# The last 256 columns of a sparse-weight matmul's output, stored in one transfer or in three

## The chip, the cores and the metric

The kernel runs on one core of a Trainium2 chip. The metric is the device time of one execution in microseconds (us). Three runs of the kernel before are at hand, and a profile of one execution.

## The reference

The weight matrix is pruned 2:4: in every group of four consecutive rows, and for each column, the two entries of largest magnitude stay and the others become zero. Then a dense layer with bias is computed for 16 x 512 = 8,192 tokens of 1,024 features.

```python
B, S, D = 16, 512, 1024             # x: [B, S, D], w: [D, D], b: [D], all bfloat16
wg = w.reshape(D // 4, 4, D)
mag = jnp.abs(wg)
order = jnp.argsort(mag, 1)
thr = jnp.take_along_axis(mag, order[:, 2:3, :], 1)
wp = (wg * (mag >= thr)).reshape(D, D)
return jnp.einsum("bsd,df->bsf", x, wp) + b
```

## The kernel before, in words

The tokens are cut into 64 tiles of 128. A tile's output is [128 tokens, 1024 columns], made in two halves of 512 columns (`FH`), each in a PSUM bank of its own; eight banks are used in turn (`next_bank`). The contraction over 1,024 features takes eight matmuls per half (`KT` = 8).

There are two stages. The front, up to line 312, runs an order written out by hand in the string `FRONT`: it loads the weights in pieces (`load_w`, line 71) and the first tokens (`load_x`, line 79) over the DMA queues of SyncE (SP in the profile, DMA queue q1) and ScalarE (ACT, DMA queue q10), prunes the weights on VectorE, and computes the first 14 tiles partly while the weights are still coming in. The main loop (line 328) then walks over batches of tiles. The tokens of a batch come from memory through a transposing DMA issued from SP (`issue_batch`, line 242), two batches ahead. Each tile takes sixteen matmuls (line 338), and VectorE adds the bias as it moves each half from PSUM to SBUF (`evac_dve`, line 219). Two tiles make a pair, and ScalarE's queue stores each finished pair with one transfer of 512 KB (`half_done`, line 199); tile 62 is stored by itself.

The last tile, 63, goes through `last_tile` (lines 317 to 326). It makes its output in four pieces, each with eight matmuls (`mm_nat`, line 234) and one bias add (line 323): columns 0 to 511, 512 to 767, 768 to 895 and 896 to 1023. The output collects in one SBUF tile, `o_last`. When 768 columns are there, ScalarE's queue stores them (line 325, 128 rows of 1,536 bytes, 192 KB). After the last piece SP's queue stores the remaining 256 columns (line 326, 128 rows of 512 bytes, 64 KB).

`K` keeps every instruction in the order in which it is written. The framework gives each transfer one of eight semaphores in rotation, and at the end of the program SP waits for all of them, and for VectorE's and ScalarE's own, before the engines meet in a closing barrier; these instructions carry line 368, the end of the program. The profile shows waits inside an engine's queue under names such as SPq and ACTq.

Of the kernel before, what the change touches and what calls it, by code (L numbers as in the profile page):

```python
# [10 lines left out]
def kernel(  # L11
# [7 lines left out]
    nc = tc.nc  # L19
    P = 128  # L20
# [5 lines left out]
    K = tc.keep_in_program_order  # L26
# [10 lines left out]
    of = out.flatten_outer_dims()  # L37
# [15 lines left out]
    def next_bank():  # L53
        bk = nbk[0] % 8
        nbk[0] += 1
        return bk
# [175 lines left out]
    def mm_nat(t, h, bk, c0=0, c1=FH):  # L232
        for kt in range(KT):
            K(nc.tensor.matmul(bank[bk][:, :c1 - c0], lhsT=xN[t][:, kt, :], rhs=wp_nat[h][:, kt, c0:c1],  # L234
                               start=kt == 0, stop=kt == KT - 1))
# [80 lines left out]

    def last_tile(t):
        o_sb = const.tile([P, Dout], bf16, name="o_last")
        for h, c0, c1 in ((0, 0, FH), (1, 0, 256), (1, 256, 384), (1, 384, FH)):
            bk = next_bank()  # L320
            mm_nat(t, h, bk, c0, c1)
            f = slice(h * FH + c0, h * FH + c1)
            K(nc.vector.tensor_tensor(o_sb[:, f], bank[bk][:, :c1 - c0], bias_sb[:, f], op=Alu.add))  # L323
            if f.stop == 768:
                K(nc.scalar.dma_start(of[t * P:(t + 1) * P, :768], o_sb[:, :768]))
        K(nc.sync.dma_start(of[t * P:(t + 1) * P, 768:], o_sb[:, 768:]))

    for bi, (t0, nb) in enumerate(batches):
        if bi + 2 < len(batches):
            issue_batch(*batches[bi + 2])  # L330
        for t in range(t0, t0 + nb):
            if t == NT - 1:
                last_tile(t)
                continue
            bks = (next_bank(), next_bank())
            for kt in range(KT):
                for h in range(2):
                    K(nc.tensor.matmul(bank[bks[h]][:], lhsT=xN[t][:, kt, :], rhs=wp_nat[h][:, kt, :],  # L338
                                       start=kt == 0, stop=kt == KT - 1))
            for _ in range(4 if t == T + F else 3):  # L340
                if later:
                    add_bias(*later.pop(0))
            for h in range(2):
                evac_dve(t, h, bks[h])
# [28 lines left out]
```

## Time and profile before

| | |
|---|---|
| three runs, median (lowest to highest) | 233.83 us (233.76 to 233.94) |
| profiled execution: span from first to last instruction | 231.53 us |
| profiled execution: its own device time | not on the page; the runs' median lies 2.30 us above the span |
| granted TensorE clock | 1.00 throughout |
| 192 KB store of line 325: issue, time to landing | 228.26 us, 1.9 us |
| 64 KB store of line 326: issue, time to landing | 229.01 us, 1.7 us |

The span counts from the first instruction to the last. What lies outside it belongs to the device time but not to the trace. "Time to landing" runs from the issue of a transfer to the last rise of its semaphore. A transfer of this kernel is spread over 16 DMA engines; each moves its share as packets, one per row, and closes with a packet of 4 bytes that raises the transfer's semaphore by one. The trace has a record of every packet with its queue, its start, its length and its size, but not with its DMA engine.

### The profile page before, as it was taken

How to read it: one execution, taken by the hardware profiler on the slowest of the kernel's cores; microseconds unless marked ns; L12 is line 12 of the kernel's file. 1: busy time of each engine (PE TensorE's matmuls, PEld its weight loads, DVE VectorE, ACT ScalarE, POOL GpSimd, SP SyncE). 2: the span in 40 equal slices, each digit the busy share in tenths (PEclk: the TensorE clock that was granted, in tenths of full speed). 3: DMA queues.
4: the chain of work that ended last, by engine and by line, in shares of the span. 5: the costliest groups of instructions: out<-in, count | busy, mean ns of one | idle time of the engine just before them, and what ended most of it. 6: DMA issues, size and time to landing. Idle time of an engine off the chain costs nothing.

```text
span 231.5 us, 2724 instructions
## 1 busy us (share of the span) xinstructions
PE 226.3 (98%) x1128; PEld 110.6 (48%) x1147; DVE 119.9 (52%) x204; ACT 18.8 (8%) x34; POOL 0.7 (0%) x6
## 2 busy tenths in 40 slices
PE   7999999999999999999999999999999999999995
PEld 3887444444444444444444444444444444444443
DVE  4899887867987424424424423423433433433433
ACT  3977500000000000000000000000000000000000
POOL 1000000000000000000000000000000000000000
DMA  6999889999847221995239822696129991122222
GB/s 194 319 200 242 190 178 178 253 246 296 295 181 272 91 83 34 239 201 172 93 75 238 230 93 91 120 258 197 63 91 197 188 249 46 47 91 91 91 93 91
DMA packets 76972, 38.19 MB, mean 165 GB/s; under 512 B 62752, under 2 KB 68896, under 8 KB 76960
## 3 DMA queue, kind: packets, MB, share of 16 engines
q1 hardware_dynamic: 67696, 20.91, 45.2%
q10 hardware_dynamic: 9264, 17.11, 20.4%
q8 instruction: 9, 0.15, 0.3%
q14 instruction: 3, 0.02, 0.0%
HBM read 3.41 MB, written 16.78 MB: 87 GB/s over the span
## 4 chain that ended last, share of the span: by engine, by line
PE 96%; DMA 2%; issue 1%; SPq 0%; DVE 0%
PE bank L338 73%; PE bank L182 16%; PE bank L234 6%; DMA xh<-in_x_dram 2%; PE bank L161 0%; SPq L79 0%; SPq L71 0%; DVE o_last L323 0%
## 5 line engine op out<-in xcount | busy, mean ns | idle before, releaser
L338 PE MATMUL bank<-wp_nat,xTb 128*128 128x512 bf16 x737 | 161.7, 379 | 0.8
L219 DVE TENSOR_TENSOR o_pair<-bank,bias_sb 128x512 bf16<-128x512 f32 x104 | 67.3, 686 | 99.6 <-PE bank L338 94.2
L338 PEld LDWEIGHTS <-xTb 128*128 128x128 bf16 x752 | 73.6, 98 | 88.7
L210 DVE TENSOR_TENSOR stage<-bank,stage 128x512 f32<-128x512 f32 x22 | 14.4, 686 | 3.9 <-PE bank L182 3.8
L182 PE MATMUL bank<-w,xT 128*128 128x256 bf16 x128 | 14.3, 273 | 0.0
L214 DVE TENSOR_TENSOR o_pair<-stage,bias_sb 128x512 bf16<-128x512 f32 x22 | 14.0, 682 | 0.0
L182 PE MATMUL bank<-wp_nat,xg 128*128 128x512 bf16 x62 | 13.9, 379 | 0.1
L182 PEld LDWEIGHTS <-xT 128*128 128x128 bf16 x128 | 12.5, 98 | 1.4
L206 ACT COPY stage<-bank 128x512 f32<-128x512 f32 x22 | 11.4, 618 | 3.9 <-PE bank L182 3.9
L182 PE MATMUL bank<-wp_nat,xfill 128*128 128x512 bf16 x47 | 10.6, 379 | 0.1
L234 PE MATMUL bank<-wp_nat,xfill 128*128 128x512 bf16 x47 | 10.5, 379 | 0.1
L182 PEld LDWEIGHTS <-xg 128*128 128x128 bf16 x64 | 6.3, 98 | 7.6
L234 PEld LDWEIGHTS <-xfill 128*128 128x128 bf16 x48 | 4.7, 98 | 5.7
L182 PEld LDWEIGHTS <-xfill 128*128 128x128 bf16 x48 | 4.7, 98 | 5.5
L338 PE MATMUL bank<-wp_nat,xTs 128*128 128x512 bf16 x32 | 7.1, 379 | 0.0
L142 DVE TENSOR_TENSOR mask<-mag,thr 128x512 bf16<-128x512 bf16 (+2 forms) x8 | 5.4, 690 | 0.2
L144 DVE TENSOR_TENSOR w<-w,mask 128x512 bf16<-128x512 bf16 (+2 forms) x8 | 5.3, 688 | 0.1
L103 PE MATMUL bank<-zeros 128*128 128x512 bf16 (+1 forms) x11 | 4.0, 533 | 1.2 <-DVE zeros L96 1.2
L338 PEld LDWEIGHTS <-xTs 128*128 128x128 bf16 x32 | 3.1, 98 | 3.8
L166 ACT COPY xT<-bank 128x512 bf16<-128x512 bf16 x8 | 4.1, 607 | 2.7 <-PE bank L161 2.7
L118 DVE TENSOR_SCALAR mag<-w 128x512 uint16<-128x512 uint16 (+2 forms) x5 | 2.3, 477 | 2.7 <-DMA w<-in_w_dram 2.7
L234 PE MATMUL bank<-wp_nat,xTb 128*128 128x128 bf16 (+2 forms) x32 | 3.7, 272 | 0.0
(20 smaller groups left out, 26.9 us busy)
## 6 DMA issues: line engine op xcount, KB each, us to landing
out_dram<-o_pair ACTq DMA_DIRECT2D x31, 512.0 KB, 2.8
wp_nat<-w SPq DMA_DIRECT2D x16, 128.0 KB, 2.8
w<-in_w_dram SPq DMA_DIRECT2D x3, 512.0 KB, 6.0
xh<-in_x_dram SPq DMA_DIRECT2D x3, 256.0 KB, 4.5
xh<-in_x_dram ACTq DMA_DIRECT2D x1, 256.0 KB, 4.0
w<-in_w_dram SPq DMA_DIRECT2D x1, 256.0 KB, 5.1
bias_sb<-in_b_dram SPq DMA_DIRECT2D x2, 128.0 KB, 3.7
out_dram<-o_pair ACTq DMA_DIRECT2D x1, 256.0 KB, 2.0
```

Of the source, the lines that this page charges most:

```text
L103: K(nc.tensor.matmul(bank[7][:, :n], lhsT=zeros[:, :P], rhs=zeros[:, :n], start=True, stop=True))
L118: K(nc.vector.tensor_single_scalar(mag[:, ms].bitcast(u16), w_of(i)[:, ms].bitcast(u16), 0x7FFF, op=Alu.bitwise_and))
L142: K(nc.vector.tensor_tensor(mask[:, ms], mag[:, ms], tb, op=Alu.is_ge))
L144: K(nc.vector.tensor_tensor(w_of(i)[:, ms], w_of(i)[:, ms], mask[:, ms], op=Alu.mult))
L166: K(nc.scalar.copy(xt[:], src))
L182: K(nc.tensor.matmul(dst, lhsT=lhs, rhs=rhs, start=c0 == 0 and m == 0, stop=c1 == FH and m == 3))
L206: K(nc.scalar.copy(stage[(h, t)][:], bank[own[(h, t)]][:]))
L210: K(nc.vector.tensor_tensor(st, bank[own[(2 + h, t)]][:], st, op=Alu.add))
L214: K(nc.vector.tensor_tensor(get_o(t)[:, f], stage.pop((h, t))[:], bias_sb[:, f], op=Alu.add))
L219: K(nc.vector.tensor_tensor(get_o(t)[:, f], bank[bk][:], bias_sb[:, f], op=Alu.add))
L234: K(nc.tensor.matmul(bank[bk][:, :c1 - c0], lhsT=xN[t][:, kt, :], rhs=wp_nat[h][:, kt, c0:c1], start=kt == 0, stop=kt == KT - 1))
L338: K(nc.tensor.matmul(bank[bks[h]][:], lhsT=xN[t][:, kt, :], rhs=wp_nat[h][:, kt, :], start=kt == 0, stop=kt == KT - 1))
```

## The change

The store of the last 256 columns, one transfer of 128 rows by 512 bytes from SP, becomes three. Columns 768 to 895 are stored from SP as soon as the third bias add is done (128 rows of 256 bytes, 32 KB). Columns 896 to 1023 are stored after the fourth bias add by two transfers of 64 tokens each (64 rows of 256 bytes, 16 KB), tokens 0 to 63 from SP and tokens 64 to 127 from ScalarE. The store of the first 768 columns stays. The matmuls, the bias adds and everything ahead of the last tile are the same.

```diff
     def last_tile(t):
         o_sb = const.tile([P, Dout], bf16, name="o_last")
+        rows = of[t * P:(t + 1) * P, :]
         for h, c0, c1 in ((0, 0, FH), (1, 0, 256), (1, 256, 384), (1, 384, FH)):
             bk = next_bank()
             mm_nat(t, h, bk, c0, c1)
             f = slice(h * FH + c0, h * FH + c1)
             K(nc.vector.tensor_tensor(o_sb[:, f], bank[bk][:, :c1 - c0], bias_sb[:, f], op=Alu.add))
             if f.stop == 768:
-                K(nc.scalar.dma_start(of[t * P:(t + 1) * P, :768], o_sb[:, :768]))
-        K(nc.sync.dma_start(of[t * P:(t + 1) * P, 768:], o_sb[:, 768:]))
+                K(nc.scalar.dma_start(rows[:, :768], o_sb[:, :768]))
+            elif f.stop == 896:
+                K(nc.sync.dma_start(rows[:, 768:896], o_sb[:, 768:896]))
+        for eng, q in ((nc.sync, slice(0, P // 2)), (nc.scalar, slice(P // 2, P))):
+            K(eng.dma_start(rows[q, 896:], o_sb[q, 896:]))
```

## The prediction

> **What bounds the kernel now.** I read the busy table first, then the chain of work that ended last, then the end of the span in the timeline, then the stretches after the last compute instruction, then the end-of-program waits, and last two places where both DMA queues were at work.
>
> The page's busy table and its chain by engine:
>
> ```profile
> PE 226.3 (98%) x1128; PEld 110.6 (48%) x1147; DVE 119.9 (52%) x204; ACT 18.8 (8%) x34; POOL 0.7 (0%) x6
> PE 96%; DMA 2%; issue 1%; SPq 0%; DVE 0%
> ```
>
> TensorE is busy for 226.3 of 231.53 us. The diff touches no matmul and no vector instruction, so only the end can move. The chain's last pieces and the timeline there (start, length, engine, line):
>
> ```profile
> 225.16 3.51 PE bank L234 x32
> 228.67 0.02 issue
> 228.69 0.29 DVE o_last L323
> ...
> 228.26 0.35 ACTq L325 DMA_DIRECT2D out_dram<-o_last  x1
> 228.69 0.29 DVE L323 TENSOR_TENSOR o_last<-bank,bias_sb 128x128 bf16<-128x128 f32 x1 [0.15 <-PE bank L234]
> 229.01 0.35 SPq L326 DMA_DIRECT2D out_dram<-o_last  x1
> ```
>
> The last bias add ends at 228.985 and SP issues the last store at 229.013. Between them and the end of the span stand 2.52 us, cut here by the store's packets (stretch, length, engines' busy time, clock, DMA share, GB/s):
>
> ```profile
> 229.01:229.86 0.84, 0.00 (x0) 0.00 (x0) 0.00 (x0) 0.00 (x0) 0.00 (x0) 1.00 0.64 233
> 229.86:230.21 0.36, 0.00 (x0) 0.00 (x0) 0.00 (x0) 0.00 (x0) 0.00 (x0) 1.00 0.63 184
> 230.21:230.70 0.49, 0.00 (x0) 0.00 (x0) 0.00 (x0) 0.00 (x0) 0.00 (x0) 1.00 0.00 0
> 230.70:231.53 0.83, 0.00 (x0) 0.00 (x0) 0.00 (x0) 0.00 (x0) 0.00 (x0) 1.00 0.00 0
> ```
>
> 0.84 us pass from issue to first packet (the busy DMA there is still ScalarE's 192 KB store), 0.36 us from the first packet to the end of the last, 0.49 us until SP sees the landing, 0.83 us for the closing barrier. The change can reach the first three, 1.69 us, and the order of the waits behind them:
>
> ```profile
> L368 SPq EVENT_SEMAPHORE  x7: 17/28/28, 229.4 to 231.5; - x7
> SPq L368 <- DMA out_dram<-o_last: 1.1, 2, 0.6
> ```
>
> By the operands in the trace's instruction records, SP's first five of these seven wait for two semaphores each: 104 and 103 (at 229.406), 107 and 102 (229.475), 108 and 100 (229.537), 109 and VectorE's (230.165), 110 and ScalarE's (230.703). Transfers take eight semaphores in rotation: 100, 102, 103, 104, 107, 108, 109, 110. The 192 KB store has 109, the last store 110, so today the last landing is looked for last.
>
> **Base.** The page gives the profiled span, 231.53, and no total of that execution; the runs' median is 233.83. The 2.30 us between lie outside the span and are taken as unchanged.
>
> **The change, part by part.** Call the unchanged 192 KB store A; B is columns 768 to 895 from SP; C1 and C2 are the token halves of the last 128 columns, from SP and ScalarE.
>
> *B.* It waits for the third bias add, whose semaphore rose at 228.553, so it issues at about 228.57 and holds SP until 228.92. Queued behind it on SP are one wait for the earlier use of semaphore 100 and then C1. A wait behind a DMA issue takes about 0.11 (229.360 to 229.475 at the end of the program), so C1 issues at about 229.03 instead of 229.013: +0.02. B's 128 packets of 256 bytes fall among A's (229.11 to 229.80). The only 256-byte packets in the trace, the transposes', took 20 ns, so eight on each of 16 engines add 0.16 us to A, whose landing at 230.15 stays 0.4 us ahead of the last one. Without that cover B would cost its own 0.16.
>
> *C2 on ScalarE.* ScalarE has issued A by 228.61 and has nothing left but its closing drain (0.15 us, at 228.65), which moves to about 229.4; SP waits until 230.7 anyway, 1.1 us of cover.
>
> *Half the packets.* Each DMA engine moved eight 512-byte packets for the last store: 0.19 us from the first packet to the engine's closing semaphore write, the engines starting over another 0.16 us. Each half has four packets to an engine: −0.09 if the second half runs alone behind the first, −0.05 if both share the engines.
>
> *Two queues at once.* This is the term that decides, and the end of the program shows no such pair. Two other places do. At the start both queues issue a transfer of the same form within 1 ns; between 1.80 and 2.44 us only one queue moved anything:
>
> ```profile
> 0.73 0.49 ACTq L71 DMA_DIRECT2D w<-in_w_dram  x1
> 0.73 0.45 SPq L71 DMA_DIRECT2D w<-in_w_dram  x1
> ...
> q1 hardware_dynamic: 75, 0.04, 24.3%
> ```
>
> SP's queue (q1) has its first packet at 1.834, ScalarE's (q10) at 2.443: 0.61 later, for transfers of 256 rows each. Later a ScalarE store meets SP's transpose, and from 91.7 to 95.0 again only q1 moves:
>
> ```profile
> 90.52 11.48 SPq L242 DMA_TRANSPOSE xTb<-in_x_dram  x1
> 91.63 0.38 ACTq L199 DMA_DIRECT2D out_dram<-o_pair  x1
> ...
> q1 hardware_dynamic: 2831, 0.72, 109.5%
> ```
>
> That store's first packet came 3.40 us after issue, against 0.90 for the same store with no transpose about. So I read one preparation stage behind both queues, taking one transfer at a time. Its time for a 64-row half has no row. Lower bound 0: the stage is pipelined and the 0.61 was the cold start. Scaled by rows, 0.61 gives 0.15. Unscaled it stays near 0.61, and first-packet times speak for a weak scaling: 0.845 for 128 rows, 0.897 for 256. With a stage of length g entered 0.35 after issue, A enters at 228.61, B at 228.92 or when A leaves, C at 229.36 or when B leaves, the other half g later. The second half is late by 0.15 for g=0.15, 0.30 for 0.30, 0.45 for 0.40, 1.08 for 0.61. I take g between 0.3 and 0.4, midway between the scaled and the unscaled reading: +0.40, ends 0 and +1.08.
>
> The Trainium skill ("DMA: Bandwidth & Descriptors", Queues, rings and completion order) says that SP and ACT have rings of their own on the same 16 engines, but no descriptor generator of their own; its Rules for kernel authors advise one 128-partition transfer in place of two partition halves, since these serialize. The two rows above agree; by that rule the sum stays as it is here, by independent queues it would be 233.98.
>
> *Landing.* From an engine's last semaphore packet to the last rise of the count took 0.36 for A (1,536-byte rows) and 0.48 for the last store (512-byte). Going on to 256-byte rows I add 0.05, ends 0 and +0.45 (a second trip of the same length, see below).
>
> *The closing waits.* The rotation goes on after 109 and 110: A 109, B 110, C1 100, C2 102. If SP's list keeps its order, the last landing is met in its second or third wait, with two or three satisfied ones after it. These stood 0.069 and 0.062 apart: +0.13 if C1 lands last, +0.20 if C2 does. I take +0.15; 0 if the list is ordered by age.
>
> Sum: 0.02 + 0.40 − 0.09 + 0.05 + 0.15 = +0.53, so 233.83 + 0.53 = **234.36 us**. About 0.2%, 0.47 us here, is what a measurement of this kernel can tell from no change; the forecast lies just beyond it.
>
> **Rivals.**
>
> *Independent queues* (not slower). Both halves start 0.85 after issue and share the engines: 0.02 + 0 − 0.05 + 0.03 + 0.15 = +0.15, 233.98, and 233.75 if the list of waits follows age and the halves land as quickly as A did. For it: no store in the last 40 us was held up at its start (0.85 to 0.90 each), and the 0.61 stands among the first DMAs of the program. Against it: the store beside the transpose. It decides if the second half's first packet comes less than 0.1 after the first's.
>
> *A long stage.* g of 0.5 to 0.61, as if a transfer cost the same whatever its size: +0.75 to +1.08 for the queueing, 0.88 to 1.21 in all, 234.7 to 235.0. Then B itself delays both halves. For it: first-packet time hardly depends on rows. Against it: the transfer has about 0.16 us between its first and last engine, as if 128 rows were laid out in that time.
>
> *A second trip for short rows.* If a 256-byte row of a 2,048-byte output row must first be fetched before it is written, the landing grows by another 0.40 to 0.48 (the trip of the last store): with little queueing (0.15) 0.02 + 0.15 − 0.09 + 0.45 + 0.15 = +0.68, 234.51. For it: the trip grew from 0.36 to 0.48 as rows shrank. Against it: that is 0.12 in a step to a third of the length. The skill's page named above (Specifications) states that transfers under 512 B are done by read-modify-write; no store of the trace has rows that short.
>
> *Faster beyond 0.47.* It would take the 1.69 us to shrink by a quarter; halving the packets gives 0.1 at most.
>
> **Chances.** Forecast case (g 0.25 to 0.45, 234.15 to 234.6) 0.42, of which 0.16 is within 0.2% and 0.26 beyond; long stage 0.20, slower; second trip 0.08, slower; independent queues 0.24, within; faster by some cut I do not see 0.06. That makes slower 0.54, within 0.40, faster 0.06. The range runs from 233.8, the lower part of the independent case, to 235.0, the end of the long stage.
>
> **What would show it.** Right: the last store's two issues at about 229.02, the first packets of one half 0.3 to 0.5 after the other's, SP's waits on L368 ending their list two or three steps after the last landing, and the stretch from the last bias add to the end of the span 3.0 us instead of 2.54. Wrong: first packets of both halves together near 229.86 (the queueing term is gone), the landing more than 0.55 behind the last packet (short rows), or the landing met in the list's last wait (the closing term).

## The result and the profile after

The change made the kernel slower: 234.17 us median against 233.70 us for the kernel before, 22 runs of each, a ratio of 1.0020 with a 95% interval of 1.0013 to 1.0027. That is 0.47 us, from 0.30 to 0.63.

The yardstick for everything below is the *tail*, from the end of the last bias add to the end of the span. It was 2.54 us before (228.985 to 231.526) and is 3.07 us after (229.349 to 232.419): +0.53 us, inside the interval of the timed runs. The profiled span itself grew by 0.89 us. The other 0.36 lies ahead of the last bias add, in instructions that the diff leaves alone. The experiments below, whose work up to there differs at most in a few transfers, moved that point between 228.89 and 229.90 us, so it is taken as the spread between executions.

The timeline at the end of the kernel after, columns as before:

```profile
228.62 0.35 ACTq L326 DMA_DIRECT2D out_dram<-o_last  x1
228.93 0.35 SPq L328 DMA_DIRECT2D out_dram<-o_last  x1
229.06 0.29 DVE L324 TENSOR_TENSOR o_last<-bank,bias_sb 128x128 bf16<-128x128 f32 x1 [0.15 <-PE bank L234]
229.38 0.56 SPq L330 DMA_DIRECT2D out_dram<-o_last  x1
229.38 0.54 ACTq L330 DMA_DIRECT2D out_dram<-o_last  x1
```

The early store (B, L328) goes out as foreseen, and both halves (L330) follow the last bias add by 0.03 us, as the single store did. But each half takes 0.54 to 0.56 us to issue, where the other stores of this stretch take 0.35. The tail cut by packets (stretch, length, engines' busy time, clock, DMA share, GB/s):

```profile
229.38:230.57 1.19, 0.00 (x0) 0.00 (x0) 0.00 (x0) 0.00 (x0) 0.00 (x0) 1.00 0.60 193
230.57:230.84 0.27, 0.00 (x0) 0.00 (x0) 0.00 (x0) 0.00 (x0) 0.00 (x0) 1.00 0.32 61
230.84:231.07 0.23, 0.00 (x0) 0.00 (x0) 0.00 (x0) 0.00 (x0) 0.00 (x0) 1.00 0.38 72
231.07:231.47 0.40, 0.00 (x0) 0.00 (x0) 0.00 (x0) 0.00 (x0) 0.00 (x0) 0.59 0.00 0
231.47:232.42 0.95, 0.00 (x0) 0.00 (x0) 0.00 (x0) 0.00 (x0) 0.00 (x0) 0.50 0.00 0
```

From the halves' issue to the first packet of ScalarE's half pass 1.19 us, where the single store took 0.84. SP's half follows 0.27 later. Its packets take 0.23, the landing and SP's step to its next wait 0.40, and the closing part from there 0.95, where it was 0.83. (The clock reads 0.59 and 0.50 in the last two rows, where TensorE has no work.) The waits at the end:

```profile
L372 SPq EVENT_SEMAPHORE  x7: 17/28/1380, 230.0 to 232.4; - x7
SPq L372 <- DMA out_dram<-o_last: 1.4, 1, 1.4
```

There is now one wait of 1.38 us. By its operands it is the second of the list, on 107 and 102, and 102 belongs to SP's half. Three satisfied waits follow it.

The +0.53 splits by the packet and landing records (times from issue): the later half's first packet 0.845 before, 1.467 after, +0.62; from there to the last closing packet 0.35 before, 0.22 after, −0.13; from there to the landing 0.48 before, 0.35 after, −0.13; from the landing to the end of the span 0.84 before, 1.01 after, +0.17. What made the first packet late is the question for the experiments.

### The profile page after: what moved, and what is told of

Its sections match the earlier page's. It is cut to its first block, busy times and chain, and to the rows that moved or that the text cites. A ratio compares the mean times of both kernels' runs of the same rounds, so it can differ in the third digit from the quotient of the medians.

```text
span 232.4 us, 2747 instructions
## 1 busy us (share of the span) xinstructions
PE 227.6 (98%) x1147; PEld 111.0 (48%) x1147; DVE 119.9 (52%) x204; ACT 18.8 (8%) x34; POOL 0.7 (0%) x6
## 4 chain that ended last, share of the span: by engine, by line
PE 96%; DMA 2%; SPq 0%; DVE 0%; issue 0%
PE bank L342 73%; PE bank L182 16%; PE bank L234 6%; DMA xh<-in_x_dram 2%; PE bank L161 0%; SPq L71 0%; SPq L79 0%; DVE o_last L324 0%
```

## The experiments

**One part alone, each.** The halves without the early store:

```diff
-            elif f.stop == 896:
-                K(nc.sync.dma_start(rows[:, 768:896], o_sb[:, 768:896]))
...
-            K(eng.dma_start(rows[q, 896:], o_sb[q, 896:]))
+            K(eng.dma_start(rows[q, 768:], o_sb[q, 768:]))
```

> Part of the change alone: columns 768 to 1023 leave in two token halves (64 rows of 512 bytes each, SP and ScalarE), with no early store of columns 768 to 895. Times from the halves' issue; the tail is from the end of the last bias add to the end of the span, 2.54 us before and 3.07 after the change. Theory 'one stage' (both queues share one preparation stage, 0.53 to 0.57 us for 128 rows, 0.27 for 64, first packet when it is done): the 192 KB store has left the stage by 0.10, so the first packets come at 0.62 and 0.89, the last landing at about 1.55, tail 2.45 to 2.60. Rival 'collision' (two queues issuing at the same instant slow each other, the early store is innocent): first packets at 1.19 and 1.47 as after the change, tail about 3.0.

Its timeline, the two halves:

```profile
229.29 0.56 SPq L328 DMA_DIRECT2D out_dram<-o_last  x1
229.30 0.56 ACTq L328 DMA_DIRECT2D out_dram<-o_last  x1
```

The first packets came 1.22 and 1.37 us after issue and the tail was 3.04; ratio 1.0017 (1.0004 to 1.0030). The halves alone cost all but 0.04 of it, though with another make-up: the second half's first packet came 0.10 sooner than after the change and its landing was met in the last wait (0.84 from there to the end, not 1.01), while its 512-byte rows took 0.54 from the last closing packet to the landing, not 0.35. 'One stage', in the form stated for this run, expected 0.62 and 0.89 and falls. The prediction's own stage, 0.3 to 0.4 us long with B out of the way, would have given about 0.85 and 1.15 to 1.25, so it does not hold either: the first half was late by as much as with B, and the second came 0.15 behind it.

The early store with a single last store:

```diff
-        for eng, q in ((nc.sync, slice(0, P // 2)), (nc.scalar, slice(P // 2, P))):
-            K(eng.dma_start(rows[q, 896:], o_sb[q, 896:]))
+        K(nc.sync.dma_start(rows[:, 896:], o_sb[:, 896:]))
```

> The other part alone: columns 768 to 895 leave early from SP, the last 128 columns in one store of 128 rows from SP. Theory 'one stage': the early store leaves the stage 0.63 after the last store's issue, the last store 0.55 later, first packet at 1.15 to 1.20, tail 2.85 to 2.95. Rival 'collision': only one queue issues at the end, first packet at 0.85, tail 2.60.

The tail was 2.52, ratio 0.9996 (0.9983 to 1.0009). The early store costs nothing. The last store took 0.41 to issue, its first closing packet came 1.01 after issue, so its first packet at about 0.87 (eight packets of 18 ns earlier), and it landed 1.57 after the last bias add, 0.13 sooner than in the kernel before. The closing waits took 0.10 of that back, since the landing on 100 was met in the third wait.

**The closing waits.** The kernel before with two idle loads, which move the rotation of semaphores by two, and the kernel after with six (the number in the code is then 6):

```diff
+            if t == 50:
+                pad = const.tile([P, 2, 64], bf16, name="pad")
+                for i in range(2):
+                    K(nc.sync.dma_start(pad[:, i, :], xf[i * P:(i + 1) * P, :64]))
             if t == NT - 1:
                 last_tile(t)
```

> The kernel before with two small loads (128 rows of 128 bytes into a tile that nothing reads) from SP at tile 50, so that the rotation of semaphores gives the last store 102 in place of 110. The stores are the same. Theory 'closing waits' (SP's list has a fixed order, 102 in its second wait): three satisfied waits follow the landing, the tail grows from 2.54 by 0.19 to 2.73. Rival (the list follows age): 2.54. In both the rest of the kernel is the same.

> The kernel after the change with six such loads, so that the two last halves get 109 and 110, the last two waits of SP's list. Theory 'closing waits': the tail shrinks from 3.07 by 0.16 to 0.20, to 2.87 to 2.91. Rival: 3.07.

The waits in SP's list, of the kernel before with moved semaphores, then of the kernel after:

```profile
L372 SPq EVENT_SEMAPHORE  x7: 17/28/1131, 230.3 to 232.4; - x7
```

```profile
L376 SPq EVENT_SEMAPHORE  x7: 17/28/28, 229.9 to 232.1; - x7
```

By the operands the last store on 102 is met in the second wait, the long one, and the time from landing to the end of the span is 1.00 us instead of 0.84. With the last half on 110, it is 0.84 instead of 1.01. So the order of the list is fixed and the place of the last landing in it is worth 0.16. The tails moved by less and by more than that, 2.54 to 2.60 (2.73 was expected) and 3.07 to 2.84 (2.87 to 2.91 was expected), because other parts moved too. In the kernel before, the same 512-byte store took 0.48 from last closing packet to landing in the one execution and 0.39 in the other; in the kernel after, the second half's first packet came 1.39 after issue instead of 1.47. The timed ratios, 0.9996 (0.9983 to 1.0010) and 1.0009 (0.9997 to 1.0020), cannot tell 0.16 us.

**Two queues, or 64 rows?** The halves can be late because two queues issue at once, or because a 64-row transfer is slow. Both halves from SP:

```diff
-        for eng, q in ((nc.sync, slice(0, P // 2)), (nc.scalar, slice(P // 2, P))):
+        for eng, q in ((nc.sync, slice(0, P // 2)), (nc.sync, slice(P // 2, P))):
```

> The change with both token halves of the last 128 columns from SP, one behind the other. Theory 'collision' (two queues issuing at the same instant slow each other): no collision here, so each issue takes 0.35 to 0.41, the first packet comes 0.85 after the first half's issue and about 1.25 for the second, the last landing 1.85 after the last bias add, tail about 2.85. Rival 'short transfers' (a transfer of 64 rows is itself slow to issue and to prepare): issues of 0.55 each, first packets at 1.2 and 1.8, tail about 3.4.

One half alone:

```diff
-        for eng, q in ((nc.sync, slice(0, P // 2)), (nc.scalar, slice(P // 2, P))):
-            K(eng.dma_start(rows[q, 896:], o_sb[q, 896:]))
+        K(nc.sync.dma_start(rows[:P // 2, 896:], o_sb[:P // 2, 896:]))
```

> The change without ScalarE's half: tokens 64 to 127 of the last 128 columns are not written. One 64-row store from SP stands alone at the end. 'Collision': issue 0.35, first packet at 0.82 to 0.85, landing about 1.45 after the last bias add, tail about 2.45. 'Short transfers': issue 0.55, first packet at 1.2, tail about 2.75.

The timelines, both halves from SP (merged into one row of two) and then the one half:

```profile
229.84 1.19 SPq L330 DMA_DIRECT2D out_dram<-o_last  x2
```

```profile
229.33 0.56 SPq L329 DMA_DIRECT2D out_dram<-o_last  x1
```

The one half cut by its packets, from issue to first packet and from there to the end of the last (the busy DMA in the first row is the two earlier stores):

```profile
229.33:230.53 1.20, 0.00 (x0) 0.00 (x0) 0.00 (x0) 0.00 (x0) 0.00 (x0) 1.00 0.59 191
230.53:230.76 0.23, 0.00 (x0) 0.00 (x0) 0.00 (x0) 0.00 (x0) 0.00 (x0) 1.00 0.37 71
```

With no other half beside it, a half takes 0.56 to issue and its first packet comes at 1.21. On one queue the second half is issued 0.61 after the first and its first packet comes 1.24 after that, tail 3.45, ratio 1.0047 (1.0032 to 1.0062); for the one half the tail is 2.75 and the ratio 1.0011 (1.0002 to 1.0020). 'Short transfers' holds on each of its numbers, and 'collision' falls as the main cause.

The last 256 columns as two stores of 128 rows were meant to give a collision without short transfers:

```diff
-        for eng, q in ((nc.sync, slice(0, P // 2)), (nc.scalar, slice(P // 2, P))):
-            K(eng.dma_start(rows[q, 896:], o_sb[q, 896:]))
+        for eng, f in ((nc.sync, slice(768, 896)), (nc.scalar, slice(896, Dout))):
+            K(eng.dma_start(rows[:, f], o_sb[:, f]))
```

> The last 256 columns in two stores of all 128 rows (256 bytes each), columns 768 to 895 from SP and 896 to 1023 from ScalarE, both after the last bias add, at the same instant; no early store. 'Collision': issues of about 0.55, first packets at 1.2 and 1.4 to 1.5, tail about 3.0. 'Short transfers': no transfer is short, issues of 0.35, both first packets at 0.85, tail 2.55 to 2.70.

It did not test this. The store of columns 768 to 895 needs the third bias add alone, so SP issued it 0.42 before the last one ended, and the kernel became the early store with the last one from ScalarE: issue 0.34, first packet at 0.85, tail 2.50, ratio 0.9994 (0.9984 to 1.0004). With the columns cut at 960, both stores need the last bias add:

```diff
+        for eng, f in ((nc.sync, slice(768, 960)), (nc.scalar, slice(960, Dout))):
```

> Two stores of all 128 rows that both need the last bias add: columns 768 to 959 from SP and 960 to 1023 from ScalarE, issued at the same instant; no early store. It measures the second queue by itself. Theory 'one stage, full rows pass quickly': issues of 0.35, the first store's first packet at 0.85, the second's 0.15 to 0.30 later, as between the two halves of the change. Rival 'the second queue costs only behind a transfer of 64 rows': both first packets at 0.85 to 0.90.

```profile
229.05 0.35 SPq L328 DMA_DIRECT2D out_dram<-o_last  x1
229.06 0.37 ACTq L328 DMA_DIRECT2D out_dram<-o_last  x1
```

Both issues are short, with first packets at 0.84 and 0.94. With 128 rows the second queue costs 0.09, less than the 0.15 to 0.27 between the halves, and between the two answers that were expected. The tail of 2.70 is 0.16 above that of the kernel before: 0.09 is this delay, and 0.08 is the landing, 0.56 from the last closing packet for the 128-byte rows where the 512-byte rows took 0.48. This kernel and the next two were run once each, so they have a trace and no timed ratio.

**Why 64 rows?** The same single last store with 32 and with 96 rows:

```diff
-        K(nc.sync.dma_start(rows[:P // 2, 896:], o_sb[:P // 2, 896:]))
+        K(nc.sync.dma_start(rows[:32, 896:], o_sb[:32, 896:]))
```

> The early store, and at the end one store from SP of tokens 0 to 31 of the last 128 columns; tokens 32 to 127 of these columns are not written. Theory 'form' (any transfer of fewer than 128 rows takes a longer way, whatever the number): issue about 0.56, first packet about 1.2 after issue, as with 64 rows. Rival 'count' (the cost grows as rows are taken away, because each DMA engine gets fewer): longer than 0.56 and later than 1.2, by the step from 128 to 64 rows about 0.67 and 1.4.

> The same with tokens 0 to 95; tokens 96 to 127 of the last 128 columns are not written. 'Form': issue 0.56, first packet 1.2. 'Count': halfway, issue about 0.46, first packet about 1.03.

The last store with 32 rows, then with 96:

```profile
228.98 0.41 SPq L329 DMA_DIRECT2D out_dram<-o_last  x1
```

```profile
228.91 0.41 SPq L329 DMA_DIRECT2D out_dram<-o_last  x1
```

Both theories fall. 32 and 96 rows issue in 0.41, like 128 rows behind the early store, and their first packets come at about 0.89 and 0.88 (first closing packet at 0.93 and 0.98, less two and six packets of 18 ns). Of the four row counts tried, 64 alone is slow. The compiled programs show a difference: the store instructions of 32, 96 and 128 rows carry a mark for a prepared issue path (`ant_dge_precooked`), and those of 64 rows do not. The last run tests the mark by taking it from a transfer of 128 rows that had it, and it repairs the change by splitting at token 96:

```diff
-            K(nc.scalar.dma_start(dst, o_pair.pop(p)[:, :n, :]))
+            nc.dge_precook = n == 2
+            K(nc.scalar.dma_start(dst, o_pair.pop(p)[:, :n, :]))
+            nc.dge_precook = True
...
-        for eng, q in ((nc.sync, slice(0, P // 2)), (nc.scalar, slice(P // 2, P))):
+        for eng, q in ((nc.sync, slice(0, 96)), (nc.scalar, slice(96, P))):
```

> Two edits that do not touch each other. First, the change with its last store split at token 96 instead of 64: 96 rows from SP, 32 from ScalarE, so that both are of forms that the compiled program marks for a short issue path, while a 64-row store has no such mark. Second, tile 62's store (128 rows, two us ahead of the 192 KB store) has the mark taken off, with the transfer itself the same. Theory 'mark' (64 rows cost because that form is issued by the long path): the two last issues take 0.35 to 0.41, their first packets come at 0.85 to 1.0 after issue, the last landing 1.5 to 1.65 after the last bias add, tail 2.55 to 2.65 with the landing met in the second wait of the list; tile 62's issue takes 0.55 instead of 0.35 and its first packet comes at about 1.2 instead of 0.85. Rival 'two queues' (a split over two queues costs whatever the rows): first packets of the last stores at 1.2 and 1.45, tail about 3.05; tile 62's store as before.

Tile 62's store in the kernel before, then this kernel's, with its last two stores:

```profile
226.31 0.35 ACTq L199 DMA_DIRECT2D out_dram<-o_pair  x1
```

```profile
226.29 0.54 ACTq L200 DMA_DIRECT2D out_dram<-o_pair  x1
...
229.00 0.41 SPq L332 DMA_DIRECT2D out_dram<-o_last  x1
229.00 0.38 ACTq L332 DMA_DIRECT2D out_dram<-o_last  x1
```

In this kernel's trace no packet moved from 226.20 to 227.45, and from there to 228.30 only ScalarE's queue moved any:

```profile
DMA packets 0, 0.00 MB, mean 0 GB/s; under 512 B 0, under 2 KB 0, under 8 KB 0
...
q10 hardware_dynamic: 143, 0.26, 82.2%
```

Without the mark the same 128 rows of 2,048 bytes take 0.54 to issue instead of 0.35, and their first packet comes at 1.20 (227.486) instead of 0.85: the numbers of the 64-row half. The opposite trial, a 64-row store with the mark, was not run. With the split at 96 the last two issues are short and the first packets come at 0.88 and about 0.89. The landing was 1.68 after the last bias add, a little later than expected (0.47 from last closing packet to landing), the tail 2.68, and the ratio 1.0002 (0.9994 to 1.0011). The tail still stands 0.14 above that of the kernel before, no more than the 0.17 that the closing waits take longer, since the last landing is on 102 again. The three stores by themselves cost nothing that the timed runs can tell; the halves of 64 rows did.

**A faster version?** The early store with one last store, and the bias loaded by one transfer, so that the last store has semaphore 110:

```diff
-            for f in (slice(0, FH), slice(FH, Dout)):
+            for f in (slice(0, Dout),):
...
+        K(nc.sync.dma_start(rows[:, 896:], o_sb[:, 896:]))
```

> The early store with one last store, as in the second experiment, and the bias loaded by one transfer instead of two, so that the last store has semaphore 110, met in the last wait of SP's list. All theories: the closing waits give back 0.16, tail 2.35 against 2.54 before; the time 0.1 to 0.2 below before, about the resolution of the timed runs.

The landing was met in the last wait, 0.835 from there to the end of the span, and the tail was 2.42, 0.12 below the kernel before (2.35 was expected). The ratio of 0.9995 (0.9986 to 1.0004) cannot show that.

## Why the prediction was right, and where it was not

The forecast was +0.53 and 234.36 us; the tail grew by 0.53 and the timed runs by 0.47. That the tail agrees to the hundredth is partly luck: the queueing term was 0.22 too low and the landing term 0.18 too high, and three smaller misses made up the rest. Of the signs that were named for it, the tail of 3.0 and the two or three waits after the last landing came true; the gap between the halves' first packets was 0.27, just short of 0.3 to 0.5, and the first half was late too, which no sign allowed for.

- *Place.* Right: only the end moved, TensorE and VectorE kept their work, and the halves issued 0.03 after the last bias add. The 0.02 for SP's queue did not appear, 0.00: SP's wait for the semaphore was through 0.02 before the bias add released it.
- *Two queues at once*, taken as +0.40. The term was mis-sized and its mechanism partly wrong. It measured +0.62: 0.36 because a 64-row store takes the long issue path, shown by the half alone (1.21 against 0.845) and by the mark, and 0.26 because the second half comes behind the first. The step that failed is the reading of one stage entered by A, B and the halves in turn. With the halves alone the first packets were nearly as late (1.22 and 1.37), and with the early store alone the last one came at about 0.87, so B was not what held them up. The two rows from which the stage was read, the 0.61 at the start and the 3.40 beside a transpose, were not tested again; at the end of the program two marked stores issued within 5 ns stood 0.09 apart.
- *A row overlooked.* The profile of before held the price of the long issue path, though no row of it told that a 64-row store would take it. SP's transfers of pruned weights (L151) mostly took 0.54 to 0.61 us to issue, and in the compiled program they lack the mark too (the row below: shortest, median and longest issue in ns). The prediction took 0.35 for every issue, from the stores of 128 rows. A long issue alone does not prove the path: two marked loads of the front, at 2.97 and 34.50 us, took 0.61 and 0.60, each directly behind an unmarked transfer on SP.

```profile
L151 SPq DMA_DIRECT2D wp_nat<-w x16: 543/602/1566, 11.7 to 33.9; - x16
```

- *B.* Its packets did not fall among A's, as the prediction had it, but behind them. The first came 1.08 after issue, 0.01 after the first of A's closing packets (229.994 and 230.006), as if each DMA engine finished its share of A before it took up B; the trace does not name the engines. As foreseen that costs nothing, since B lands 0.7 ahead of the last half.
- *Half the packets*, −0.09: measured −0.13.
- *Landing*, +0.05: measured −0.13, the wrong sign. The rival of a second trip for short rows falls: rows of 256 bytes took 0.35 to 0.47 in all runs, rows of 512 bytes 0.39 to 0.54. The 0.48 of the profile of before was a high value; the same store took 0.39 in the third experiment. The Trainium skill ("DMA: Bandwidth & Descriptors", Specifications) states that transfers below 512 bytes are done by read-modify-write. No run here shows whether they are; the trip to the landing did not grow at 256 bytes, and the 0.56 of the 128-byte rows, seen once, is just above the range of the 512-byte rows.
- *Closing waits*, +0.15: measured +0.17, and the place in the list is shown to matter in both directions. The halves had their semaphores the other way round than foreseen, SP's 102 and ScalarE's 100, and SP's landed last, so three waits followed.
- *Independent queues* asked for a gap below 0.1. Between the halves it was 0.15 to 0.27, so it falls for this change; for 128 rows, 0.09, it would have held. Its lower end does not come out of its own terms: with the list by age and a landing as quick as A's, 0.02 − 0.05 − 0.12 gives 233.68, not 233.75. *A long stage* falls with the stage.

What stays open: why the second of two halves comes 0.15 to 0.27 later, a second 128-row store only 0.09 and the 96 and 32 rows within about 0.01 of each other; and why the compiled program marks stores of 32, 96 and 128 rows but not of 64.

## What to carry to other kernels

Before you split a transfer to make it shorter, look up what the issue of the new form costs, in the row of a transfer of that form and not of a larger one; where no row has the form, as here, a trial of that transfer alone tells it. At the end of this kernel the issue and the way to the first packet (0.85 us for 128 rows, 1.21 for 64) outweighed the packets themselves (0.2 to 0.4 us from the first to the last). Compare issue times over all transfers in a profile, since one value of 0.35 and another of 0.56 can point to two paths, and a slightly different split can take the short one. A sum that comes out right is checked term by term, for two of these terms were wrong by about 0.2 us in opposite directions.

## What was not expected of the hardware

- The stores at the end of this kernel issue on one of two paths. On the marked one they took 0.34 to 0.41 us and, apart from the early store behind A, had the first packet 0.84 to 0.94 after issue, for 32, 96 and 128 rows; on the unmarked one 0.54 to 0.58 and 1.19 to 1.24, 1.37 to 1.47 for the second of two halves issued at once. Taking the mark from a transfer of 128 rows moved it from the one to the other (0.35 and 0.85 to 0.54 and 1.20).
- SP meets landings in a fixed order of semaphores at the end of the program: the last landing in the second wait instead of the fifth was worth 0.16 us.
